# Three engines put into program order behind a matmul stream: chunk attention and a gated MLP on one core

## The chip, the core and the metric

The kernel runs on one core of a Trainium2 chip. The core has a matrix engine (TensorE, in the profile PE, its weight loads PEld), a vector engine (VectorE, DVE), an activation engine (ScalarE, ACT), a general one (GpSimd, POOL) and one that here only issues transfers (SyncE, SP; its queue is SPq). Each takes its instructions in the order of its own list; semaphores tie the lists together. Matmuls read SBUF and write PSUM. The metric is the device time of one execution in microseconds (us).

## What is computed

The inputs are q, k and v (8 batches, 8 heads, 576 tokens, head size 64), two weights of 512 x 1536, one of 1536 x 512 and a norm's gain g of 512.

```python
# attention inside chunks of 64 tokens, per head
scores = q_c @ k_c.T / sqrt(64); scores -= max(scores)
attn = exp(scores) / (sum(exp(scores)) + 1e-9)
x = attn @ v_c                        # as [4608 tokens, 512]
# root mean square norm and gated MLP
xn = x / sqrt(mean(x * x) + 1e-6) * g
h = silu(xn @ w_gate) * (xn @ w_val)  # [4608, 1536]
out = h @ w_out                       # [4608, 512]
```

All is float32. Every wide product is made of three matmuls of a reduced form: an operand is split into a high half (a cast) and a low half (operand minus high half), and high x high, high x low and low x high are summed. So each operand costs a cast (ScalarE) and a subtraction (VectorE).

## The kernel before, in words

The 4608 tokens are 9 tiles of 512; attention goes by units of 256 tokens, so two units make a tile, four a pair of tiles. Tiles 0, 1 and 2 are done plainly: for each f of 12 (128 columns of the middle size) `gated` makes the gate and the value product (`up`, 24 matmuls), silu on ScalarE (line 523), the product on VectorE (line 527), the high half gh (line 528) and the low half gl (line 532); then `down` of the f before adds 12 matmuls into four accumulators. The other 6 tiles are three pairs, done by a scheme with seven products instead of eight, named P1 to P7: `up_pair` runs 6 times per pair, with 7 products of 12 matmuls each; `after` evacuates each product (copies on ScalarE, sums on VectorE, products on GpSimd). `down_pair` then runs 42 pieces (7 products x 6) of 6 matmuls; each piece needs a split of its token operand, gh on ScalarE (line 829) and gl on VectorE (line 830), made by `split_next` one piece ahead.

The attention of later tiles lies between these matmuls. A unit is a list of steps (`unit_steps`): load q, k, v; scores on TensorE (line 244) with the softmax (`turned_softmax`: a reduction and a subtraction, each twice per half unit, and the exp); sums, a transposition on VectorE and a store (`turn`); the load that brings the tiles home turned (`turn_back`, the tile eT); the values on TensorE (line 366) and the norm (`turned_norm`, with the square and its sum on ScalarE, `inv_rms` with the power -1/2 on GpSimd, line 433, and the scale on ScalarE, line 388); the turned x to memory (`turn_x`, line 394) and back (`turn_x_back`). `Steps` holds a table: at which step which of these functions runs. Tile two has 24 half steps (two per f), a pair has 84 (42 products up, 42 pieces down); the constants UNIT_AT, UNIT_STEPS, PAIR_AT, PAIR_STEPS place the units. The same tables hold `out_sides` (in tile two: sums and splits of the output weights for the pairs, stored to memory) and `x_sides` (scale by g, line 676, sums, line 679, and splits, lines 662 and 663, of a pair's x into the seven operands xp). Weights of the pairs come from memory as tiles wr (up, three ahead) and wo (down, three ahead), through SP's queue like every transfer.

What sets the order: from tile one on a manual schedule holds TensorE's list in program order (line 1012). The lists of ScalarE, VectorE, GpSimd and SP come from a scheduler that goes by priority and its own estimates; `urgent()` lifts the priority of an evacuation or a split.

Buffers that matter: `io` has 4 (q, k, v of a unit and its xu), `gp` 2 each for gh and gl, `tmp` 4, `xs` 8, `wts` 18 large ones (xp, wr, wo, g, tt), PSUM two banks each for `ps_h` and `ps_a`, four for `ps_acc`.

## Time and profile before

| | |
|---|---|
| median of 3 runs | 935.68 us (932.73 to 936.3) |
| profiled execution, its own time | 935.86 us |
| span from first to last instruction | 934.0 us |
| mean granted clock of TensorE | 0.993 |
| tile two, 258.24 to 375.73 | 117.5 us |
| first pair, 375.73 to 567.01 | 191.3 us |
| second pair, 567.01 to 756.64 | 189.6 us |
| third pair (no attention left), 756.64 to the end | 177.4 us |
| transfers | 231.85 MB, mean 248 GB/s |

The stretches are read from TensorE's rows: each starts with its first wide matmul. A row of the timeline gives start, length, engine, line, operation, the tiles (written <- read), shapes and a count of merged instructions; a bracket at its end tells how long the engine sat idle before it and what ended that. A row of the table of waits gives engine, line and tile, what it waited for, the total in us, how often and the longest.

### The profile page before, as it was taken

The numbers are of one execution on the slowest core, as the hardware profiler recorded it, in microseconds if no ns is written. First come the engines' busy times: TensorE is split into PE (matmuls) and PEld (weight loads), VectorE is DVE, ScalarE is ACT, GpSimd is POOL, SyncE is SP. The second block draws the span as 40 slices with busy tenths as digits, with TensorE's granted clock in tenths as the row PEclk, the third lists the DMA queues.
The fourth block names the chain that finished last, engine by engine and source line by source line (L and its number), as shares of the span: only waits on it lengthen the run. The fifth ranks groups of instructions, "written<-read, shape, count | busy, mean of one in ns | idle before, by whom it ended". The sixth has DMA issues, their size and how long they took to land.

```text
span 934.0 us, 17571 instructions
## 1 busy us (share of the span) xinstructions
PE 892.4 (96%) x6828; PEld 726.1 (78%) x6828; DVE 637.0 (68%) x1065; ACT 470.8 (50%) x779; POOL 186.7 (20%) x161
## 2 busy tenths in 40 slices
PE   5699989999999989999998999999999999999997
PEld 4478868888888778888886888888877888888786
DVE  5899983654578783975775996666859954333775
ACT  4989853443456543744453654354636632322453
POOL 0100012224300000143333001443320013332201
PEclk9999999999999999999999999999999999999999
DMA  8688998778876766677796686777777675345801
GB/s 343 243 316 303 331 325 281 244 252 249 294 288 230 229 183 202 250 276 262 237 323 241 240 331 210 283 260 241 267 273 258 241 273 229 135 153 206 340 23 69
DMA packets 85795, 231.85 MB, mean 248 GB/s; under 512 B 8912, under 2 KB 45264, under 8 KB 71504
## 3 DMA queue, kind: packets, MB, share of 16 engines
q1 hardware_dynamic: 85712, 230.72, 70.3%
q8 instruction: 54, 0.88, 0.4%
q14 instruction: 29, 0.24, 0.1%
HBM read 167.25 MB, written 63.44 MB: 247 GB/s over the span
## 4 chain that ended last, share of the span: by engine, by line
PE 76%; issue 7%; ACT 6%; DVE 6%; POOL 2%; DMA 1%; SPq 0%; DVEq 0%; ACTq 0%; POOLq 0%
PE ps_c L722 11%; PE ps_a L722 11%; PE ps_b L722 10%; PE ps_g L505 7%; PE acc L540 7%; PE ps_v L505 7%; PE ps_b L911 5%; PE ps_d L722 5%; PE ps_c L911 4%; PE ps_d L911 3%; PE ps_a L911 3%; PE ps_o L366 2%; PE ps_s L244 2%; DVE gl L830 1%; ACT w L157 1%
## 5 line engine op out<-in xcount | busy, mean ns | idle before, releaser
L722 PE MATMUL ps_b<-xp,wr 128*128 128x512 f32 x432 | 106.0, 395 | 0.0
L722 PE MATMUL ps_c<-xp,wr 128*128 128x512 f32 x432 | 104.6, 391 | 0.0
L505 PE MATMUL ps_g<-xh,parts 128*128 128x512 f32 x288 | 98.1, 400 | 5.9 <-ACT sg L523 5.1
L722 PE MATMUL ps_a<-xp,wr 128*128 128x512 f32 x432 | 103.5, 390 | 0.0
L505 PE MATMUL ps_v<-xh,parts 128*128 128x512 f32 x288 | 96.0, 393 | 0.0
L722 PEld LDWEIGHTS ps_b<-xp,wr 128*128 128x128 f32 x432 | 81.7, 190 | 17.4
L722 PEld LDWEIGHTS ps_a<-xp,wr 128*128 128x128 f32 x432 | 80.9, 188 | 16.9
L722 PEld LDWEIGHTS ps_c<-xp,wr 128*128 128x128 f32 x432 | 80.6, 188 | 17.0
L540 PE MATMUL acc<-parts,gh 128*128 128x512 f32 x288 | 90.8, 396 | 0.0
L829 ACT CAST gh<-g 128x512 fp32r<-128x512 f32 x72 | 44.6, 623 | 51.8 <-DVE gl L830 21.0
L505 PEld LDWEIGHTS ps_g<-xh,parts 128*128 128x128 f32 x288 | 55.0, 191 | 19.5 <-ACT sg L523 6.4
L505 PEld LDWEIGHTS ps_v<-xh,parts 128*128 128x128 f32 x288 | 54.7, 190 | 11.5
L540 PEld LDWEIGHTS acc<-parts,gh 128*128 128x128 f32 x288 | 53.5, 189 | 11.6 <-ACT parts L182 0.2
L801 POOL TENSOR_TENSOR g<-u,u 128x512 f32<-128x512 f32 x18 | 23.2, 1289 | 185.8 <-ACT u L769 72.1
L830 DVE TENSOR_TENSOR gl<-g,gh 128x512 fp32r<-128x512 f32 x72 | 49.3, 700 | 12.2 <-ACT gh L829 11.9
L505 PE MATMUL ps_g<-xl,parts 128*128 128x512 f32 x144 | 57.0, 396 | 0.0
L540 PE MATMUL acc<-parts,gl 128*128 128x512 f32 x144 | 56.4, 392 | 0.0
L505 PE MATMUL ps_v<-xl,parts 128*128 128x512 f32 x144 | 56.4, 392 | 0.0
L791 POOL TENSOR_TENSOR p<-p,p 128x512 f32<-128x512 f32 x36 | 46.9, 1318 | 42.8 <-DVE p L790 33.5
L769 ACT ACTIVATE p<-p 128x512 f32<-128x512 f32 x36 | 22.6, 632 | 64.4 <-POOL p L791 61.2
L433 POOL TENSOR_TENSOR ri<-ss,mhalf 128x1 f32<-128x1 f32 x32 | 19.6, 623 | 173.6 <-DVE ss L431 173.5
L527 DVE TENSOR_TENSOR sg<-ps_v,sg 128x512 f32<-128x512 f32 x36 | 24.7, 686 | 42.0 <-PE ps_v L505 35.0
(141 smaller groups left out, 1794.9 us busy)
## 6 DMA issues: line engine op xcount, KB each, us to landing
wr<-wsd SPq DMA_DIRECT2D x63, 1024.0 KB, 6.8
wo<-osd SPq DMA_DIRECT2D x30, 1024.0 KB, 7.8
raw<-w_up_dram SPq DMA_DIRECT2D x12, 1024.0 KB, 9.6
vt<-v_dram SPq DMA_DIRECT2D x18, 512.0 KB, 5.2
wsd<-parts SPq DMA_DIRECT2D x18, 512.0 KB, 7.0
qt<-qT_dram SPq DMA_DIRECT2D x17, 512.0 KB, 4.9
kt<-kT_dram SPq DMA_DIRECT2D x17, 512.0 KB, 5.8
away_e<-e SPq DMA_DIRECT2D x28, 256.0 KB, 2.4
```

The costliest lines, as they stand in the source:

```text
L244: nc.tensor.matmul(st["s"][j][c * CH : (c + 1) * CH, pr], st["q"][rows, pr, tok : tok + CH], st["k"][rows, pr, tok : tok + CH], start=True ...
L433: nc.gpsimd.tensor_tensor(ri, ss, mhalf, op=ALU.pow)
L505: nc.tensor.matmul(ps, a[f][:, cols], b[dt], start=(dt == 0 and i == 0), stop=(dt == NDT - 1 and i == 2),)
L527: nc.vector.tensor_tensor(sg, pv, sg, op=ALU.mult)
L540: nc.tensor.matmul(acc[s], a[:, cols], b, start=(f == 0 and i == 0), stop=(f == NF - 1 and i == 2),)
L722: nc.tensor.matmul(ps, w[:, a, m, cols], xp[:, b, kt], start=start and kt == 0 and i == 0, stop=stop and kt == 1 and i == 2, skip_group_ch ...
L769: nc.scalar.activation(t, t if src is None else src, AF.Silu)
L791: nc.gpsimd.tensor_tensor(kp["p5"], kp["p1"], kp["p5"], op=add)
L801: nc.gpsimd.tensor_tensor(g[:, 0, 1], kp["u2"], kept[0]["u2"], op=mult)
L829: nc.scalar.copy(gh, src)
L830: nc.vector.tensor_tensor(gl, src, gh.bitcast(F32), op=ALU.subtract)
L911: nc.tensor.matmul(banks[m][name], w[:, a, m * P : (m + 1) * P], b, start=opens and i == 0 and k == 0, stop=not (opens and p != P4) and i ...
```

## The change

From tile two on the manual schedule covers TensorE, ScalarE, VectorE and SP (not GpSimd); tile one keeps TensorE alone. So what the text says last runs last on each of these engines, and the tables of steps are dealt anew in smaller pieces:

- a unit has 12 steps: the two exps stand together behind both softmaxes (one step later in the pairs), the halves of a unit go away and come home separately, and the norm is three steps: the product with the square sums of both halves (`turned_norm`), the root (`turned_root`: one VectorE and one GpSimd instruction on two columns instead of two on one), the scale (`turned_scale`);
- in tile two the first half step of an f runs inside `gated`, between the high and the low half of that f; `out_sides` comes in four smaller lists from step 0 on; the load of the pairs' first weights goes from half step 14 to 18; the first unit's load goes to the end of tile one;
- `x_sides` is dealt as single casts and subtractions; the scale by g goes from VectorE to ScalarE; the operands P3, P6, P7 and P4 (and in tile two P5's low half) are made in the first four products of the pair that uses them;
- the two sums at the end of `up_pair` run behind the second product of the next one, the last ones behind piece 1 of the down phase;
- the down phase's high halves are made two pieces ahead, in `tmp` tiles, the low halves one ahead; the first two high halves and the first low one inside the last up product; the copy of P2's result goes to an `xs` tile; at the last piece of a product the matmuls go by bank, first all of one, then all of the other;
- `urgent()` goes where the order is now that of the text.

```diff
 UNIT_AT = 1, 5, 9, 13
-UNIT_STEPS = -2, 0, 1, 3, 5, 6, 7
-FIRST_STEPS = -2, 0, 1, 3, 7, 8, 9
-PAIR_STEPS = -4, 0, 3, 5, 8, 11, 13
-PAIR_AT = 2, 12, 21, 31
+UNIT_STEPS = -3, 0, 0, 1, 1, 2, 2, 5, 6, 6, 7, 8
+FIRST_STEPS = -2, 0, 0, 1, 1, 3, 3, 7, 7, 7, 8, 9
+PAIR_STEPS = -4, 0, 1, 2, 3, 4, 4, 8, 9, 10, 11, 12
+PAIR_AT = 3, 12, 22, 31
+OUT_AT = 3
+X_AT = 5, 12, 13, 14, 15, 16, 25, 27, 30
+IN_ORDER = {
+    mybir.EngineType.PE,
+    mybir.EngineType.Activation,
+    mybir.EngineType.DVE,
+    mybir.EngineType.SP,
+}
...
+    def turned_exp(i):
+        e = state[i]["e"]
         nc.scalar.activation(e, e, AF.Exp, scale=SCALE)
...
+    def turned_norm(u):
+        xu = state["xu", u] = io.tile([P, 4, NDT, 2, Q], F32, tag="io", name="xu")
+        xv = xu.rearrange("p q a s d -> p s (q a) d")
+        ss = state["ss", u] = small.tile([P, 2], F32, name="ss_u")
+        for s in range(2):
+            st = state.pop(2 * u + s)
+            nc.vector.tensor_tensor(
+                xv[:, s].rearrange("p (h b) d -> p h b d", b=2),
+                st["o"].rearrange("p (h b d) -> p h b d", b=2, d=Q),
+                st["rs"].rearrange("p h (o i) -> p h o i", i=1).broadcast_to([P, H, 2, Q]),
+                op=ALU.mult,
+            )
+            spent = st["eT"].rearrange("p t h q -> p (t h) q")
+            nc.scalar.activation(spent, xv[:, s], AF.Square, accum_out=ss[:, s : s + 1])
+    def turned_root(u):
+        ss = state["ss", u]
+        nc.vector.tensor_scalar(ss, ss, 1.0 / DM, 1e-6, op0=ALU.mult, op1=ALU.add)
+        ri = state["ri", u] = small.tile([P, 2], F32, name="ri_u")
+        nc.gpsimd.tensor_tensor(ri, ss, mhalf.broadcast_to([P, 2]), op=ALU.pow)
+    def turned_scale(u):
+        xv = state["xu", u].rearrange("p q a s d -> p s (q a) d")
+        ri = state.pop(("ri", u))
+        for s in range(2):
+            nc.scalar.mul(xv[:, s], xv[:, s], ri[:, s : s + 1])
...
+        if between is not None:
+            between()
         with urgent():
             nc.vector.tensor_tensor(gl, sg, gh.bitcast(F32), op=ALU.subtract)
         return gh, gl
...
+        return [
+            [join, sums_one],
+            [lambda: split(P7, (2, 1)), sums_two],
+            [lambda: split(P5, (2, 2)), lambda: split(P6, (1, 1))],
+            [lambda: split(P3, (1, 2))],
+        ]
     def save_plain(i):
...
+        def high(p):
+            xside[p] = big([P, 2, 2, TT], F32R, "xp")
+            hi, _, x = views(p)
+            nc.scalar.copy(hi, x)
+        def low(p):
+            hi, lo, x = views(p)
+            nc.vector.tensor_tensor(lo, x, hi.bitcast(F32), op=ALU.subtract)
...
         def scale(x, dts):
             for dt in dts:
                 col = g_col[:, dt : dt + 1]
-                nc.vector.tensor_scalar(x[:, :, dt], x[:, :, dt], col, None, op0=ALU.mult)
+                nc.scalar.mul(x[:, :, dt], x[:, :, dt], col)
...
+        late = [
+            [lambda: less(got["t1"], b22, got["t1"]), lambda: high(P3), lambda: high(P6)],
+            [lambda: low(P6), lambda: less(b12, b22, b12), lambda: low(P3), lambda: high(P7)],
+            [lambda: low(P7), lambda: less(b21, got["t1"], b21), lambda: high(P4)],
+            [lambda: low(P4)],
+        ]
+        return one, two, late
     ring = {}
...
                 product(n, m, p, b, p in (P1, P6, P5, P4), p in (P2, P7, P3, P4))
-            with urgent():
-                after(p, ps, kept, g)
+            if k == 6 and last is not None:
+                last()
+            after(p, ps, kept, g)
+            if k == 1 and sums:
+                sums.pop()()
             step()
...
+        def sum_up():
+            nc.vector.tensor_tensor(t, g[:, 0, 1], g[:, 0, 0], op=ALU.subtract)
+            nc.vector.tensor_tensor(g[:, 0, 1], g[:, 1, 1], g[:, 0, 1], op=ALU.subtract)
+        sums.append(sum_up)
...
+    def split_high(src, ready):
+        gh = tmp.tile([P, TT], F32R, tag="tmp", name="gh")
+        nc.scalar.copy(gh, src)
+        ready.append([gh])
+    def split_low(src, pair):
+        gl = gp.tile([P, TT], F32R, name="gl")
+        nc.vector.tensor_tensor(gl, src, pair[0].bitcast(F32), op=ALU.subtract)
+        pair.append(gl)
...
+        def next_high(n):
+            if n < len(order):
+                split_high(source(n), ready)
+        def next_low(n):
+            if n >= len(order):
+                return
+            split_low(source(n), ready[n])
...
-            split_next(n + 1)
-            gh, gl = ready.pop(n)
+            next_high(n + 2)
+            next_low(n + 1)
+            gh, gl = ready[n]
             w = wos[n // PER][:, n % PER]
-            for k, (a, b) in enumerate(((0, gh), (1, gh), (0, gl))):
-                for m in range(2):
-                    nc.tensor.matmul(
-                        banks[m][name],
-                        w[:, a, m * P : (m + 1) * P],
-                        b,
-                        start=opens and i == 0 and k == 0,
-                        stop=not (opens and p != P4) and i == NPR - 1 and k == 2,
-                        skip_group_check=True,
-                    )
+            todo = [(m, k) for k in range(3) for m in range(2)]
             if i == NPR - 1:
-                with urgent():
-                    finish(p, banks, kept)
+                todo.sort()
+            for m, k in todo:
+                nc.tensor.matmul(
+                    banks[m][name],
+                    w[:, (0, 1, 0)[k], m * P : (m + 1) * P],
+                    (gh, gh, gl)[k],
+                    start=opens and i == 0 and k == 0,
+                    stop=not (opens and p != P4) and i == NPR - 1 and k == 2,
+                    skip_group_check=True,
+                )
+            if i == NPR - 1:
+                finish(p, banks, kept)
+            if n == 1:
+                sums.pop()()
             step()
     def unit_steps(u, x):
...
+        def second():
+            turned_softmax(both[1])
             for i in both:
-                turned_softmax(i)
-
-        def second():
-            for i in both:
-                turned_sum(i)
-                turn(i)
-
-        def third():
-            for i in both:
-                turn_back(i)
-
-        def fourth():
+                turned_exp(i)
...
             lambda: load_unit(u),
             first,
             second,
-            third,
-            fourth,
+            lambda: away(both[0]),
+            lambda: away(both[1]),
+            lambda: turn_back(both[0]),
+            lambda: turn_back(both[1]),
+            values,
+            lambda: turned_root(u),
+            lambda: turned_scale(u),
             lambda: turn_x(u),
             lambda: turn_x_back(u, x),
         ]
...
+            at.setdefault(21, []).append(lambda: load_unit(2 * PLAIN))
         elif t == 2:
+            ordered.__exit__(None, None, None)
             st = last.open("st2", 1)
             x2 = st.tile([P, NSUB, DM], F32, tag="x2", bufs=1, name="x2")
-            at = {}
+            ordered = tc.manual_schedule(engines=IN_ORDER)
+            ordered.__enter__()
             for n, u in enumerate(range(2 * PLAIN, 2 * PLAIN + 4)):
                 for k, f in enumerate(unit_steps(u, (x, x2)[n // 2])):
-                    at.setdefault(max(UNIT_AT[n] + UNIT_STEPS[k], 0), []).append(f)
+                    if n or k:
+                        at.setdefault(UNIT_AT[n] + UNIT_STEPS[k], []).append(f)
...
+            one, two, late = x_sides(x, x2, st)
+            for n, f in enumerate(one):
                 at.setdefault(15 + n, []).append(f)
-            for n, f in enumerate(x_both):
-                at.setdefault(22 + n // 6, []).append(f)
-            at.setdefault(14, []).append(lambda: ring_load_ahead(0))
-            half = Steps(at)
+            at.setdefault(23, []).extend([two[0], two[4], *two[1:3]])
+            late = [[two[3]] + late[0], *late[1:]]
+            at.setdefault(18, []).append(lambda: ring_load_ahead(0))
+            early = {n: list(todo) for n, todo in enumerate(late)}
...
+            one, two, late = x_sides(x, x2, st)
+            for n, f in enumerate(one[:2]):
+                at.setdefault(PAIR_AT[1] + PAIR_STEPS[-1] + 2 + n, []).append(f)
+            for n, f in zip(X_AT, one[2:] + two[:1] + two[4:] + two[1:4]):
+                at.setdefault(7 * NPR + n, []).append(f)
+            early = {n: list(todo) for n, todo in enumerate(late)}
         step = Steps(at)
         gts, wos, tt = [], [], []
+        sums, ready = [], []
+        def first_splits():
+            for g, _ in gts[:2]:
+                split_high(g[:, 0, 0], ready)
+            split_low(gts[0][0][:, 0, 0], ready[0])
         for i in range(NPR):
-            gts.append(up_pair(i, step, wos, tt))
+            last_part = first_splits if i == NPR - 1 else None
+            gts.append(up_pair(i, step, wos, tt, sums, last_part))
         loaded[0] = 0
-        down_pair(t, gts, wos, step, b + 1 < NB)
+        down_pair(t, gts, wos, step, b + 1 < NB, sums, ready)
     ordered.__exit__(None, None, None)
     last.close()
```

More of the change, by code (lines that the diff above doesn't have):

```diff
@@ L512, in up, with gated @@
         return ps
-    def gated(f, at, then):
+    def gated(f, at, then, between=None):
         pg = up(wgh, wgl, f, "ps_g")
@@ L655, in big @@
         return wts.tile(shape, dtype, tag="wts", name=name)
-    def x_side(p, src):
-        t = xside[p] = big([P, 2, 2, TT], F32R, "xp")
-        hi, lo = (t[:, i].rearrange("p k (n c) -> p k n c", c=2 * Q) for i in range(2))
-        src = src.rearrange("p n k c -> p k n c")
-        nc.scalar.copy(hi, src)
-        nc.vector.tensor_tensor(lo, src, hi.bitcast(F32), op=ALU.subtract)
     xside = {}
@@ L732, in hold, with up_pair @@
         return xs.tile([P, TT], F32, tag="xs", name=name)
-    def up_pair(i, step, wos, tt):
+    def up_pair(i, step, wos, tt, sums, last=None):
         g = big([P, 2, 2, TT], F32, "g")
@@ L837, in out_load, with down_pair, source @@
         return t
-    def down_pair(t, gts, wos, step, more):
+    def split_high(src, ready):
[6 more added lines that the diff above has]
+        pair.append(gl)
+    def down_pair(t, gts, wos, step, more, sums, ready):
         order = [(p, i) for p in DOWN for i in range(NPR)]
-        ready = {}
         add, sub = ALU.add, ALU.subtract
-        def split_next(n):
-            if n >= len(order):
-                return
+        def source(n):
             p, i = order[n]
             g, tt = gts[i]
-            src = {
+            return {
                 P1: g[:, 0, 0], P5: tt, P2: g[:, 1, 0], P6: tt,
@@ L853, in split_next @@
             }[p]
-            ready[n] = split_g(src)
+        def next_high(n):
[5 more added lines that the diff above has]
+            split_low(source(n), ready[n])
+            p, i = order[n]
+            g, tt = gts[i]
             if p == P5:
@@ L875, in finish @@
                 elif p == P2:
-                    o = tmp_tile("o")
+                    o = hold("o")
                     nc.scalar.copy(o, b["a"])
@@ L931, in first, with away, values @@
                 scores(i, sc)
+            turned_softmax(both[0])
+        def second():
+            turned_softmax(both[1])
             for i in both:
[L933 to L944 removed]
+                turned_exp(i)
+        def away(i):
+            turned_sum(i)
+            turn(i)
+        def values():
             turned_values(u)
[L946 to L947 removed]
+            turned_norm(u)
         return [
```

103 lines of the change are left out of this document (33 added, 70 removed).

## The prediction

> **What bounds the kernel now.** I read the page first, then TensorE's timeline from tile two on, the table of waits for that stretch, and last the rows of the other engines around each stall.
>
> ```profile
> span 934.0 us, 17571 instructions
> PE 892.4 (96%) x6828; PEld 726.1 (78%) x6828; DVE 637.0 (68%) x1065; ACT 470.8 (50%) x779; POOL 186.7 (20%) x161
> ```
>
> TensorE is busy for 892.4 of 934.0 us, so the change can only win what TensorE loses. What a stretch should cost I take from a place without stalls. A row gives its start, its length, the engine, the line and the count.
>
> ```profile
> 572.29 2.88 PE L722 MATMUL ps_c<-xp,wr 128*128 128x512 f32 x12
> 575.10 1.16 PE L244 MATMUL ps_s<-kt,qt 64*64 64x64 f32 x64
> 576.19 3.02 PE L722 MATMUL ps_b<-xp,wr 128*128 128x512 f32 x12
> ...
> 598.18 1.48 PE L366 MATMUL ps_o<-vt,eT 64*32 64x64 f32 x128
> 599.59 3.02 PE L722 MATMUL ps_c<-xp,wr 128*128 128x512 f32 x12
> ```
>
> Twelve wide matmuls start at 572.29 and the next thing at 575.10, so twelve cost about 2.72 us when others follow at once: the same pitch as six in 1.36. The scores of a unit take 576.19 - 575.10 = 1.09 us, its values 599.59 - 598.18 = 1.41 us. All this work stays. What is not in this beat are the waits; each row of their table has the total in us, the count and the longest.
>
> ```profile
> PE ps_a L911 <- DVE gl L830: 6.0, 7, 1.6
> PE ps_o L366 <- DMA eT<-away_e: 1.9, 2, 1.6
> ...
> PEld ps_a L911 <- DVE gl L830: 9.5, 8, 2.1
> ```
>
> Nearly all the waiting from 258 us on is of two kinds: the first split halves of a down phase (gl, line 830) and the values of a unit (line 366). VectorE and ScalarE are not full over the span (68% and 50%). They are late at places, by the order in which their work was laid out.
>
> **Part one: values that come too late.** Each pair of rows gives the start of the values (or of what they delay) and of the work behind them.
>
> ```profile
> 307.85 0.27 PE L366 MATMUL ps_o<-vt,eT 64*32 64x64 f32 x2 [0.33 <-DMA eT<-away_e]
> 310.86 0.73 PE L540 MATMUL acc<-parts,gh 128*128 128x512 f32 x2
> ...
> 328.88 0.27 PE L366 MATMUL ps_o<-vt,eT 64*32 64x64 f32 x2
> 333.05 1.22 PE L540 MATMUL acc<-parts,gh 128*128 128x512 f32 x2
> 337.34 0.50 PE L505 MATMUL ps_g<-xh,parts 128*128 128x512 f32 x1 [0.59 <-ACT sg L523]
> ...
> 351.17 2.58 PE L366 MATMUL ps_o<-vt,eT 64*32 64x64 f32 x128
> 353.68 0.73 PE L540 MATMUL acc<-parts,gh 128*128 128x512 f32 x2
> ...
> 495.03 1.47 PE L366 MATMUL ps_o<-vt,eT 64*32 64x64 f32 x127
> 498.76 4.42 PE L722 MATMUL ps_b<-xp,wr 128*128 128x512 f32 x12
> 503.02 2.90 PE L722 MATMUL ps_d<-xp,wr 128*128 128x512 f32 x12
> ...
> 656.43 2.19 PE L366 MATMUL ps_o<-vt,eT 64*32 64x64 f32 x128
> 658.54 3.01 PE L722 MATMUL ps_b<-xp,wr 128*128 128x512 f32 x12
> ```
>
> Against 1.41 us the values at 307.85 take 3.01, at 328.88 4.17, at 351.17 2.51, at 495.03 3.73, at 656.43 2.11. Lost: 1.60 + 2.76 + 1.10 + 2.32 + 0.70 = 8.5 us. Twice the twelve matmuls behind are slow too: 333.05 to 337.34 is 4.29 us (with a 0.59 wait inside), 498.76 to 503.02 is 4.26 us, against 2.72: 1.57 + 1.54 = 3.1 us. In the second case the clock shows it (the third-last column is the granted clock):
>
> ```profile
> 494.00:504.00 10.00, 7.97 (x150) 6.21 (x149) 4.65 (x9) 2.25 (x6) 2.77 (x3) 0.83 0.83 347
> ```
>
> The change brings the tiles of a unit home earlier: in tile two turn_back comes 2 half steps after the scores instead of 3, with the values left at 5; in the pairs the store of the first half comes at 2 instead of 3 steps, turn_back at 4 instead of 5, with the values left at 8. One pair step is 2.72 us, a half step of tile two about 4.1 us (8.16 / 2). The largest lateness above is 2.76 us. So I book all 8.5 us and the 3.1 us of slow clock that follow from them as won.
>
> **Part two: the first pieces of a down phase.**
>
> ```profile
> 694.27 1.07 PE L911 MATMUL ps_a<-gh,wo 128*128 128x512 f32 x4
> ...
> 706.32 1.07 PE L911 MATMUL ps_c<-gh,wo 128*128 128x512 f32 x4
> ...
> 508.11 1.24 DVE L394 STREAM_TRANSPOSE xu<-xu 128x1024 f32<-128x1024 f32 x1
> 510.44 2.31 DVE L663 TENSOR_TENSOR xp<-x,xp 128x1024 fp32r<-128x1024 f32 x1
> ```
>
> The first product of the down phase has six pieces of six matmuls, 8.16 us by the beat; from 694.27 to 706.32 it takes 12.05. Meanwhile VectorE works at 510.44 (the same place one pair earlier) on an operand of the next pair, an instruction that the scheduler put between two splits, after the turned x at 508.11. The change makes the first two high halves and the first low half inside the last up product, always keeps the high half two pieces ahead and the low half one, and leaves on VectorE among the first six pieces only the subtraction of line 803, the last unit's turned x (1.24) and two sums. A low half is due 0.91 us into its piece of 1.36. With 0.65 us for every subtraction (1.29 for the two of line 890, below), piece 1's is ready at 0.65 + 0.65 = 1.3 of 2.27 us, piece 2's, behind the turned x, at 3.2 of 3.63, piece 3's, behind the sums, at 5.2 of 4.99: 0.2 us late, say 0.4 with the handing over, in the two phases that have units. TensorE's own waits of this kind are 6.0 us, those of its weight queue 9.5 us; the loss at 694.27 alone is 3.89 us, so the truth is near the upper one: 9.0 us won. The 0.4 in two phases, 0.8 us, goes to what is added; if VectorE comes 1 us late in each of three phases it is 3.0.
>
> **Part three: the tail.**
>
> ```profile
> 928.42 0.61 PE L911 MATMUL ps_d<-gl,wo 128*128 128x512 f32 x2
> 928.92 1.29 DVE L890 TENSOR_TENSOR p<-p,ps_d 128x512 f32<-128x512 f32 x2 [1.67 <-PE ps_d L911]
> ```
>
> Both last subtractions wait for the last matmul. Sorting the last piece by bank closes the first bank three matmuls (0.68 us) earlier; the one behind it then has only itself to wait for. 0.7 us won; the store behind it is unchanged.
>
> **Part four: moved work that should cost nothing.** The scale by g goes from VectorE to ScalarE, 24 instructions (minimum, median and maximum in ns):
>
> ```profile
> L676 DVE TENSOR_SCALAR x<-x,g_col x24: 432/480/1520, 332.5 to 717.7; 128x512 f32<-128x512 f32 x24
> L388 ACT ACTIVATE xu<-xu,ri x28: 707/722/727, 198.9 to 694.6; 128x512 f32<-128x512 f32 x28
> ```
>
> VectorE loses 24 x 0.48 = 11.5 us, ScalarE gets 24 x 0.72 = 17.3 us. It lies in the down phases and at the end of tile two; ScalarE, busy for half the span, covers it; without cover the price is at most 17.3 us, of which 5.8 are more than VectorE paid. [...] The delayed sums, the split of out_sides and the high half in another pool add no instruction and no transfer. The two exps of a unit now stand together, which saves table loads at best; booked at zero.
>
> **Part five: what program order adds.** Now an engine whose head waits holds everything behind it.
>
> ```profile
> 258.00:376.00 118.00, 114.32 (x1204) 93.05 (x1203) 84.18 (x179) 60.64 (x102) 5.24 (x8) 0.99 0.69 221
> ...
> L315 DVE TENSOR_TENSOR e<-ps_s,mx 128x256 f32<-128x256 f32 x56 | 21.0, 412 | 0.0
> L679 DVE TENSOR_TENSOR t<-x,x 128x1024 f32<-128x1024 f32 x3 | 3.7, 1218 | 0.0
> ```
>
> In tile two VectorE is busy for 84.18 of 118 us, but unevenly: the softmax of a unit is 4 x (0.41 + 0.41) = 3.3 us (the reduction taken like the subtraction) at one half step, and between half steps 6 and 14 softmax, away, norm and out_sides of several units meet, while the first and last f have one unit or none. I estimate 46 us of VectorE's 84 in the five f from 3 to 7, where TensorE needs 5 x (8.16 + 2.50 / 2) = 47. There a wait of VectorE isn't made good. turned_root and turned_scale stand in one half step: ScalarE holds scale until POOL's root is done (0.55 to 1.0 us), works 2 x 0.72, and only then makes the copy on which VectorE's next split waits: about 2.5 us idle. Behind ScalarE's scale stands the next silu, on that the PSUM bank of TensorE. The first and last unit have slack; for two units I book 2 x 2.5 = 5.0 us. The bounds are 0 and 4 x 2.5 = 10.0; no gain below zero, as the waits of before are already booked. At the start of a pair the late operands come in: before P6 (5.44 us after P1, as P2 and P5 lie between) VectorE has t1's difference (1.22), a product that waits for a silu behind two casts, and P6's low half (1.22). That ends about when it is due: 0.4 us for each of three, 1.2 us; bounds 0 and 3 x 1.22 = 3.7. SP's moved transfers cost nothing while weights are three tiles ahead.
>
> **Sum.** The profiled execution took 935.86 us, 1.86 more than its span and 0.18 more than the median of 935.68. Won: 8.5 + 3.1 + 9.0 + 0.7 = 21.3. Added: 5.0 + 1.2 + 0.8 = 7.0. 935.86 - 21.3 + 7.0 = 921.6, so 922.
>
> **Rivals.** *Nothing is added:* the waits fit in the slack and the time is 935.86 - 21.3 = 914.6. For it: VectorE is busy for 68% of the span; against: the 46 of 47 us above.
>
> *ScalarE waits for the root in order (slower).* The root is now one instruction on two columns per unit, not two on one.
>
> ```profile
> 126.55 3.94 POOL L470 TENSOR_TENSOR ri_u<-ss_u,mhalf 128x2 f32<-128x2 f32 x1 [41.45 <-DVE ss_u L468]
> ...
> 129.25 0.69 DVE L167 TENSOR_SCALAR w<-w 128x1024 int32<-128x1024 int32 x1
> ...
> 130.53 0.72 ACT L472 ACTIVATE x<-x,ri_u 128x512 f32<-128x512 f32 x1 [4.50 <-POOL ri_u L470]
> ...
> L433 POOL TENSOR_TENSOR ri<-ss,mhalf x32: 543/551/1951, 17.1 to 693.9; 128x1 f32<-128x1 f32 x32
> ```
>
> This two-column case took 3.94 us and ended at 130.49, 0.55 us after VectorE's row at 129.25, which stands without idle time behind its forerunners; ScalarE's scale waited 4.50 us with a silu behind it. Against it stand 32 single-column ones with a median of 0.55 us. If twelve units from tile two on pay this, the four of tile two cost 4.5 us each and the eight in the pairs, where scale comes one step (2.72 us) later, 1.8 each: 32.4 us, 954. The time is slower by 0.5% (940.4) from (940.4 - 921.6) / 12 = 1.6 us per unit. [...]
>
> *SP's queue.* Four io buffers hold q, k, v and xu. In tile two the load of a unit now comes two half steps before the turned x of the unit two earlier has left, and its v finds no buffer. The text order can't be kept strictly there, as the transfer that frees the buffer stands behind it.
>
> ```profile
> eT<-away_e SPq DMA_DIRECT2D x112, 64.0 KB, 3.3
> away_x<-xu SPq DMA_DIRECT2D x14, 512.0 KB, 3.7
> ```
>
> If turn_back stands behind that v, it starts after 3.7 us of the other transfer and lands 3.3 us on, at a point where two half steps (8.2 us) are all there is: about 2.5 us late for three units, plus 1.5 us of slow clock each, 12 us: 934. That would be no change.
>
> **How the numbers follow.** This kernel's three runs span 0.4%, so 0.5% (4.7 us) is about what can be told from nothing: under 931.0 is faster, over 940.4 slower. Forecast 0.58, nothing added 0.20, SP's queue 0.12, the root 0.10. So faster 0.78, same 0.12, slower 0.10. The range reaches down past 914.6 by the few us by which unquoted small waits could add, to 911, and up past 931 (21.3 won, 10.0 + 3.7 + 3.0 added) and the SP case to 936, which leaves the slower case out.
>
> **What would show it.** Right: no wait of a down phase's first pieces on gl; values of 1.41 us throughout; no stretch of granted clock under 0.9 after 258 us; ScalarE's scale waiting for POOL and VectorE for the split's cast in tile two, with TensorE waiting there for a few us in all; tile two still over its beat, the pairs nearly on it. Wrong: waits of 4 us at the scale, weights (wr, wo) among TensorE's waits, or the values still late.

## The result and the profile after

The changed kernel takes 957.07 us (median of 4 runs, 953.39 to 959.79) against 935.1 in the same session: ratio 1.0239, 95% interval 1.0217 to 1.0261, 2.4% slower. The profiled execution took 954.95 us. Its page, the span, the engines and the start of the chain of work that ended last:

```profile
span 953.2 us, 17568 instructions
PE 897.7 (94%) x6828; PEld 726.7 (76%) x6828; DVE 640.1 (67%) x1027; ACT 460.8 (48%) x787; POOL 180.8 (19%) x147
PE 58%; DMA 12%; DVE 11%; issue 8%; ACT 7%; SPq 2%; POOL 1%; DVEq 0%; ACTq 0%; POOLq 0%
```

No engine has noticeably more to do; TensorE executes the same 6828 matmuls. The chain tells more: DMA is now 12% of it (1% before). TensorE's waits from 258 us on:

```profile
PE ps_o L377 <- DVE e L323: 6.9, 4, 5.5
PE ps_b L757 <- DMA wr<-wsd: 4.3, 3, 2.0
PE ps_s L252 <- issue: 4.1, 3, 1.7
PE ps_o L377 <- DMA away_x<-xu: 3.2, 1, 3.2
...
PEld ps_a L964 <- DVE gl L880: 4.8, 8, 0.8
```

The first pieces of the down phases wait less for gl (weight queue 4.8 against 9.5). The values (line 377) still wait, now behind the softmax (line 323); weights (wr) and scores without a named cause are new. The granted clock is the third-last column here: it dipped to 0.96 in tile two, the first stretch.

```profile
254.73:383.15 128.42, 115.57 (x1202) 93.39 (x1200) 79.85 (x164) 54.14 (x99) 2.78 (x4) 0.96 0.56 186
383.15:581.71 198.56, 189.96 (x1525) 152.47 (x1524) 140.42 (x222) 95.56 (x157) 45.83 (x36) 0.98 0.70 255
581.71:776.47 194.76, 188.16 (x1525) 151.35 (x1524) 138.10 (x220) 92.12 (x151) 45.85 (x36) 0.99 0.70 257
776.47:953.20 176.73, 172.42 (x757) 141.40 (x755) 102.59 (x137) 60.94 (x100) 44.08 (x32) 1.00 0.49 185
```

Where the time went follows from TensorE's rows: each group from its start to the next one's, less the prediction's beat. Loss above the beat in us (the two right columns are experiments told below):

| | before | after | TensorE alone in order (3) | the best kernel (17) |
|---|---|---|---|---|
| tile two | 9.4 | 20.4 | 2.8 | 6.1 |
| first pair, up | 5.9 | 14.9 | 17.5 | 4.6 |
| first pair, down | 4.0 | 2.3 | 1.8 | 2.8 |
| second pair, up | 3.1 | 10.8 | 5.5 | 1.8 |
| second pair, down | 5.1 | 2.6 | 3.9 | 3.9 |
| third pair with its tail | 6.1 | 5.3 | 5.6 | 5.6 |
| sum from tile two on | 33.6 | 56.3 | 37.1 | 24.8 |

22.7 us are lost net. (Up to the end of tile zero all kernels told of here run the same code, and yet tile one begins at 149.5 to 157.5 us in their profiles. So I count from tile two on. A stage starts here with the start of its first wide matmul; the table ahead of the change took the end of the matmul before it for the pairs, about 0.16 us later, hence 117.5 there and 117.3 below.)

In tile two it begins on SyncE's queue. These rows of the timeline are from all engines, unrelated ones left out:

```profile
297.18 0.38 SPq L221 DMA_DIRECT2D kt<-kT_dram  x1
...
301.75 1.16 PE L252 MATMUL ps_s<-kt,qt 64*64 64x64 f32 x64
...
302.98 0.33 SPq L222 DMA_DIRECT2D vt<-v_dram  x1
...
303.71 0.56 SPq L624 DMA_DIRECT2D osd<-side  x1
...
304.37 3.76 SPq L360 DMA_DIRECT2D eT<-away_e  x8
...
307.86 0.41 ACT L622 CAST side<-wo 128x256 fp32r<-128x256 f32 x1 [3.38 <-DMA osd<-side]
...
308.30 0.43 DVE L623 TENSOR_TENSOR side<-wo,side 128x256 fp32r<-128x256 f32 x1 [3.32 <-ACT side L622]
...
309.24 0.42 DVE L322 TENSOR_REDUCE mx<-ps_s 128x4 f32<-128x256 f32 x1
...
311.80 0.27 PE L377 MATMUL ps_o<-vt,eT 64*32 64x64 f32 x2 [3.21 <-DMA away_x<-xu]
312.06 0.42 DVE L323 TENSOR_TENSOR e<-ps_s,mx 128x256 f32<-128x256 f32 x1
312.59 1.82 PE L377 MATMUL ps_o<-vt,eT 64*32 64x64 f32 x126 [0.52 <-DVE e L323]
```

The queue stands from 297.6 to 302.98: v finds no buffer until the unit's own scores have freed one. It happens to two units of tile two, for 11.1 us in all. In the queue's own waits this is in two rows, one for the time until q has landed and one for the time until the scores have read it:

```profile
SPq L222 <- PE ps_s L252: 5.8, 2, 3.2
SPq L222 <- DMA qt<-qT_dram: 5.3, 2, 2.8
```

Behind v stand a store (osd) and the turn-back. ScalarE's cast needs the buffer of a stored part and waits 3.38 us, VectorE's subtraction waits for the cast, and the softmax, whose scores were done at 301.75 + 1.09 = 302.84, begins at 309.24. The values of the unit before need the two banks that the softmax reads: two of their 128 matmuls start at 311.80, the others at 312.59, 0.11 us after the softmax's last subtraction (312.06 + 0.42). The store that the row at 311.80 names carries another unit's x; the values don't read it.

In the pairs the same queue, up to the wide matmuls that wait:

```profile
502.43 7.60 SPq L360 DMA_DIRECT2D eT<-away_e  x8
510.12 0.37 SPq L749 DMA_DIRECT2D wr<-wsd  x1
...
515.15 4.12 PE L757 MATMUL ps_b<-xp,wr 128*128 128x512 f32 x10 [2.02 <-DMA wr<-wsd]
```

A weight load stands 7.6 us behind eight turn-backs.

### The profile page after: what moved, and what is told of

Read it like the earlier page. It is cut to its first block, busy times and chain, and to the rows that moved or that the text cites. A ratio compares the mean times of both kernels' runs of the same rounds, so it can differ in the third digit from the quotient of the medians.

```text
span 953.2 us, 17568 instructions
## 1 busy us (share of the span) xinstructions
PE 897.7 (94%) x6828; PEld 726.7 (76%) x6828; DVE 640.1 (67%) x1027; ACT 460.8 (48%) x787; POOL 180.8 (19%) x147
## 4 chain that ended last, share of the span: by engine, by line
PE 58%; DMA 12%; DVE 11%; issue 8%; ACT 7%; SPq 2%; POOL 1%; DVEq 0%; ACTq 0%; POOLq 0%
PE acc L564 6%; PE ps_b L757 6%; PE ps_c L757 6%; PE ps_a L757 6%; PE ps_g L527 6%; PE ps_v L527 5%; PE ps_c L964 5%; PE ps_b L964 5%; DMA wr<-wsd 5%; PE ps_a L964 4%; PE ps_d L757 4%; PE ps_d L964 2%; DMA osd<-side 2%; PE ps_o L377 1%; DMA away_e<-e 1%
## 5 line engine op out<-in xcount | busy, mean ns | idle before, releaser
L880 DVE TENSOR_TENSOR gl<-g,gh 128x512 fp32r<-128x512 f32 x72 | 52.2, 731 | 18.8 <-PE ps_c L964 6.0
L527 PE MATMUL ps_v<-xl,parts 128*128 128x512 f32 x144 | 56.3, 391 | 0.0
L811 ACT ACTIVATE p<-p 128x512 f32<-128x512 f32 x36 | 22.7, 632 | 68.4 <-POOL p L833 47.9
L757 PE MATMUL ps_d<-xp,wr 128*128 128x512 f32 x216 | 52.7, 393 | 2.8 <-DVE u L839 1.8
```

Source lines behind the costliest of these rows:

```text
L527: nc.tensor.matmul(ps, a[f][:, cols], b[dt], start=(dt == 0 and i == 0), stop=(dt == NDT - 1 and i == 2),)
L757: nc.tensor.matmul(ps, w[:, a, m, cols], xp[:, b, kt], start=start and kt == 0 and i == 0, stop=stop and kt == 1 and i == 2, skip_group_ch ...
L811: nc.scalar.activation(t, t if src is None else src, AF.Silu)
L880: nc.vector.tensor_tensor(gl, src, pair[0].bitcast(F32), op=ALU.subtract)
```

## The experiments

"All in order" means TensorE, ScalarE, VectorE and SyncE's queue. Ratios are to the kernel before on the same chip. Stage times are from one profiled execution each, whose span stands beside the median; that of 10 took 6.5 us less than its median, that of 13 4.9 us more.

| kernel | median us | ratio, 95% interval | span | tile two | pair 0 | pair 1 |
|---|---|---|---|---|---|---|
| before | 935.1 | | 934.0 | 117.3 | 191.3 | 189.6 |
| after | 957.07 | 1.0239 (1.0217 to 1.0261) | 953.2 | 128.4 | 198.6 | 194.8 |
| 1 SyncE free | 942.34 | 1.0079 (1.0052 to 1.0107) | 944.7 | 115.4 | 201.2 | 190.4 |
| 2 VectorE, ScalarE free | 940.82 | 1.0059 (1.0033 to 1.0084) | 938.5 | 113.8 | 198.0 | 191.4 |
| 3 all three free | 935.68 | 1.0005 (0.9984 to 1.0025) | 937.0 | 110.7 | 200.6 | 190.8 |
| 4 v and turn-backs later | 976.9 | 1.043 (1.0392 to 1.0467) | 978.2 | 118.2 | 215.7 | 213.1 |
| 5 v later | 950.15 | 1.0172 (1.0137 to 1.0208) | 951.5 | 118.1 | 200.7 | 198.9 |
| 6 v later, four wr ahead | 953.1 | 1.0193 (1.0153 to 1.0234) | 954.3 | 118.5 | 206.1 | 194.6 |
| 7 as 3, tile two's units earlier | 936.51 | 1.0019 (1.0001 to 1.0036) | 934.4 | 113.6 | 200.0 | 188.7 |
| 8 as 3, pair units 2, 12, 22, 32 | 934.6 | 0.9998 (0.9979 to 1.0016) | 932.4 | 111.1 | 197.6 | 191.4 |
| 9 osd stores on GpSimd | 950.35 | 1.014 (1.0096 to 1.0184) | 952.3 | 120.5 | 202.7 | 196.8 |
| 10 v later in tile two | 950.1 | 1.0141 (1.0092 to 1.019) | 941.9 | 118.2 | 195.4 | 198.3 |
| 11 as 10, four wr ahead in up | 938.41 | 1.0046 (1.0016 to 1.0077) | 936.9 | 118.1 | 193.8 | 191.1 |
| 12 as 7, operands in tile two | 932.31 | 0.9964 (0.9942 to 0.9985) | 933.8 | 114.0 | 192.0 | 189.2 |
| 13 as 11, q and k earlier | 936.92 | 1.003 (1.0002 to 1.0058) | 940.0 | 115.1 | 200.4 | 192.4 |
| 14 as 13, pair units 2, 12, 22, 32 | 935.86 | 0.9998 (0.9975 to 1.0022) | 932.4 | 115.1 | 192.9 | 191.0 |
| 15 as 13, scale later | 936.52 | 1.0026 (0.9994 to 1.0058) | 934.8 | 112.8 | 193.7 | 191.7 |
| 16 as 12, pair units 2, 12, 22, 31 | 929.0 | 0.9934 (0.9905 to 0.9963) | 927.8 | 114.3 | 189.5 | 188.8 |
| 17 as 12, pair units 1, 11, 21, 31 | 924.93 | 0.9897 (0.987 to 0.9925) | 922.4 | 114.0 | 188.9 | 187.1 |
| 18 as 15, pair units 2, 12, 22, 31 | 934.8 | 1.0008 (0.9979 to 1.0038) | 932.1 | 112.8 | 193.8 | 191.8 |

### Which order costs (1 to 4)

```diff
 IN_ORDER = {
     mybir.EngineType.PE,
-    mybir.EngineType.Activation,   # 2 and 3
-    mybir.EngineType.DVE,          # 2 and 3
-    mybir.EngineType.SP,           # 1 and 3
 }
```

Expected of 1, SyncE free:

> SyncE's queue is taken out of the set of engines in program order; everything else is the changed kernel (957.07). Theory Q (SyncE's queue in program order is the cause: a load of v with no buffer, and turn-back loads that wait for a store, hold the queue, and the stores, weights and inputs behind them come late): the waits of ps_b and ps_c for wr go, the values in tile two are 1.41 us again, tile two falls from 128.4 to about 116 and pairs 0 and 1 from 198.6 and 194.8 to about 190: 921 to 932. Rival H (the order of VectorE and ScalarE is the cause: softmax, scales and evacuations stand behind others that wait): the late values stay, 945 to 957.

Expected of 2, VectorE and ScalarE free:

> VectorE and ScalarE are taken out of the set; TensorE and SyncE's queue stay in program order. Theory Q: most of the loss stays, 947 to 960, with wr among TensorE's waits. Rival H: the loss goes, 925 to 938.

Expected of 3, all three free:

> Only TensorE is in program order, as before, with the new step tables and the finer pieces. It stands beside the one without SyncE: the difference of the two is what the order of VectorE and ScalarE brings by itself. Theory Q: 921 to 937, no wr waits. Rival H: also 921 to 937, but then the kernel without SyncE alone must be far above it. A third theory (the new steps, not the order, lose the time) says about 955 here.

The order of SyncE's queue alone costs 940.82 - 935.68 = 5.1 us, that of VectorE and ScalarE alone 6.7, both together 21.4: 9.6 more than the sum. 1 and 2 each ended between what Q and what H had said, and neither theory holds alone. Theory Q is half right: the queue has to be held and VectorE and ScalarE have to be unable to go round what it holds. Rival H alone is out (VectorE and ScalarE in order without SyncE: 942.34, not 945 and more), and kernel 3 rules out the new steps as the cause (935.68, not 955). But the new steps bring nothing either: tile two is 6.6 us shorter than before and pair 0 9.3 longer. The rows of kernel 3 there:

```profile
368.79 5.60 PE L754 MATMUL ps_a<-xp,wr 128*128 128x512 f32 x24
377.27 0.51 PE L754 MATMUL ps_c<-xp,wr 128*128 128x512 f32 x1 [2.88 <-ACT xp L700]
378.66 5.06 PE L754 MATMUL ps_c<-xp,wr 128*128 128x512 f32 x11 [0.88 <-DVE xp L704]
383.52 3.65 PE L754 MATMUL ps_b<-xp,wr 128*128 128x512 f32 x12
```

P5 (ps_c) is due at 374.23 and starts at 377.27; from there to the next product pass 6.25 us, 0.88 of them a wait, where the beat is 2.72. With P6 7.4 us are lost at once.

Kernel 4 keeps all in order, moves v's load behind the unit's own scores (from unit 6 on) and both turn-backs of a pair's unit:

```diff
-PAIR_STEPS = -4, 0, 1, 2, 3, 4, 4, 8, 9, 10, 11, 12
+PAIR_STEPS = -4, 0, 1, 2, 3, 6, 6, 8, 9, 10, 11, 12
...
-        nc.sync.dma_start(vt, v[u])
...
             for i in both:
                 scores(i, sc)
+            load_values(u)
```

Expected of 4:

> SyncE's queue stays in program order, but two things that stop it are moved: from unit 6 on the load of v is issued behind the unit's own scores instead of with q and k, and in the pairs the two turn-backs come at step 6 instead of 4. Theory Q: nothing else is needed, tile two about 117 and the pairs about 190, so 922 to 935. Rival H: no change, 950 to 957. If only the length of the queue counts and not what stops it, it also stays above 945.

A miss by 42 us, and useful: tile two came down by 10.2 us, the pairs rose by 17 and 18. TensorE's largest wait there:

```profile
PE ps_o L383 <- DMA eT<-away_e: 22.4, 16, 4.2
```

Here a step of the ordered queue was a place, not a time: two steps later was two steps of weights later, and the turned rows missed the values.

### The two moves apart, and the given-back gain (5 to 8)

5 is kernel 4 without the line of PAIR_STEPS, 6 adds a tile of lead; 7 and 8 are kernel 3 with one line each.

```diff
-AHEAD_R = 3                    # 6
+AHEAD_R = 4
-UNIT_AT = 1, 5, 9, 13          # 7
+UNIT_AT = 0, 4, 8, 12
-PAIR_AT = 3, 12, 22, 31        # 8
+PAIR_AT = 2, 12, 22, 32
```

Expected of 5:

> All three queues in program order, with one edit: from unit 6 on the load of v is issued behind the unit's own scores. In the kernel with both moves tile two came down from 128.4 to 118.2 us and the pairs rose to 215.7 and 213.1, with 22.4 us of values that waited for turned rows. Theory V (v's load that finds no buffer is what costs tile two its 11 us; the turn-backs at step 6 alone cost the pairs theirs): tile two about 118, pair 0 about 198, pair 1 about 195 as in the changed kernel, 945 to 949. Rival (v behind the scores is itself what makes the pairs late): pairs near 215, about 975.

Expected of 6:

> As the kernel with only v's load moved, and the weights of the pairs' up phase are loaded four tiles ahead instead of three. Theory W (in the pairs a wr load stands behind a turn-back that waits up to 7.9 us for its store, and three tiles of lead do not cover it): TensorE's waits for wr, 5.9 us in all in the changed kernel, and the slow clock behind them go, 937 to 942. Rival R (the loads then only stand elsewhere in the same queue: the fourth tile finds no buffer and holds the queue itself): no gain over the kernel with only v moved, 945 to 955.

Expected of 7:

> Only TensorE in program order, and the four units of tile two one half step (4.7 us) earlier. With only TensorE in order tile two fell to 110.7 us and pair 0 began with 7.4 us of waits for its P5 operands, whose tokens came back at about 373. Theory C (the chain of tile two's last unit, not TensorE, sets when pair 0 can go on, so what tile two gains pair 0 gives back): the waits at pair 0's start fall by 4 to 5 us or go, 929 to 932. Rival (a half step earlier meets VectorE and ScalarE at the same work and gains nothing, or the values in tile two come late): 934 to 938.

Expected of 8:

> Only TensorE in program order, and the units of a pair at steps 2, 12, 22, 32 instead of 3, 12, 22, 31, so that two steps lie between the values of one unit and the scores of the next in every case, not in one of three. Theory I (scores that come one step behind the values stall in their middle because TensorE's next block of instructions is only then being fetched: 1.9 us without a releaser, a 16 KB instruction packet at 414.5 and at 474.3): scores take 1.09 us throughout, 3 to 6 us less in the two pairs, 930 to 933. Rival (the stall is a wait for the banks that the values hold, or for q and k): it stays, 934 to 938.

Tile two is 118.1 us in 5: theory V holds there, though only 6.9 of its 10 us reach the end; the last units' values stalled (4.3 and 5.8 us over the beat in the two pairs). In 6 TensorE never waits for wr, but for wo, which now stands behind four wr of the next pair; rival R holds there. TensorE's largest wait of 6, and its queue at the end of a down phase:

```profile
PE ps_d L970 <- DMA wo<-osd: 7.3, 2, 4.3
```

```profile
561.28 2.11 SPq L755 DMA_DIRECT2D wr<-wsd  x4
563.49 0.61 SPq L876 DMA_DIRECT2D wo<-osd  x1
```

7 is a miss: the operands of P5 came no earlier. Its transfers from 350 to 370 us (KB each, median us from issue to landing) show why: the turned x landed after 11.2 us, beside 3.7 us for it in the prediction's row.

```profile
away_x<-xu SPq DMA_DIRECT2D x1, 512.0 KB, 11.2
```

Three wr tiles had been issued right ahead of it:

```profile
348.54 1.40 SPq L746 DMA_DIRECT2D wr<-wsd  x3
349.99 0.83 SPq L416 DMA_DIRECT2D away_x<-xu  x1
```

In 8 the stalled scores went (5.2 us to none) as theory I has it, and first pieces of down waited 7.8 us for gl instead.

### The way from the held queue to TensorE (9 to 12)

```diff
-            nc.sync.dma_start(out_home(i, p), part...)      # 9
+            nc.gpsimd.dma_start(out_home(i, p), part...)
-            lambda: load_unit(u),                           # 10, 11: v later in tile two alone
+            lambda: load_unit(u, not 2 * PLAIN <= u < 2 * PLAIN + 4),
-        while loaded[0] < min(n + AHEAD_R, len(wsd)):       # 11, with AHEAD_R = 4
+        while loaded[0] < min(n + (AHEAD_R if n else 3), len(wsd)):
-            at.setdefault(18, []).append(lambda: ring_load_ahead(0))   # 12
+            at.setdefault(14, []).append(lambda: ring_load_ahead(0))
-            at.setdefault(23, []).extend([two[0], two[4], *two[1:3]])
+            at.setdefault(22, []).extend([two[0], two[4], *two[1:4], *late[0]])
+            at.setdefault(23, []).extend([*late[1], *late[2], *late[3]])
```

Expected of 9:

> The changed kernel, all three queues in program order, v's load where it was; only the stores of the down weights' parts (osd) are issued by GpSimd instead of SyncE. Theory S (the held queue costs tile two through these stores: the parts keep their buffers, ScalarE's next cast waits up to 5.5 us for a store, VectorE's subtraction and the softmax stand behind it): the casts no longer wait, tile two falls from 128.4 to about 118, 945 to 949. Rival E (the held queue costs through the turned rows that come late to the values): the values still wait, tile two above 125, 953 to 958.

Expected of 10:

> The changed kernel with v's load behind the scores in tile two's four units alone; the pairs as changed. Tile two 118 as in the two kernels that moved v in all units; pairs 198.6 and 194.8 as changed, without the 8.2 us of values without a releaser that those had at the fourth unit: 945 to 949. If that wait has another cause than v's place, 950 as with v moved everywhere.

Expected of 11:

> As the kernel with v moved in tile two alone, and four tiles of weights ahead in the up phase only, three at the change from down to up, so that down's own last tiles keep their buffers (with four there, wo came 7.3 us late at the ends of the down phases). Theory W: neither wr nor wo is waited for, pair 0 about 195 and pair 1 about 190, 937 to 943. Rival R (the fourth tile's load holds the queue for a buffer): another load or the turned rows come late, 945 to 952.

Expected of 12:

> Only TensorE in program order, tile two's units one half step earlier as before, and now the work that turned out to stand by its place in the program: the pairs' first weights are loaded at half step 14 as in the kernel before (18 in the changed one), and the token operands for P5, P6, P3, P7 and P4 are made at half steps 22 and 23 instead of in pair 0's first steps. Theory C2 (what tile two gains is given back at pair 0's start, 7.4 us, because these operands are placed there and their tokens wait in the DMA queues behind 4 MB of weights, q and k): the waits for xp at pair 0's start go, pair 0 about 193, 928 to 931. Rival (VectorE and ScalarE have no room at tile two's end, so the wait moves to tile two's last steps): 934 to 937.

9 leaves v where it holds the queue and takes only the stores out from behind it. ScalarE's wait for them in tile two, after and in 9:

```profile
ACT side L622 <- DMA osd<-side: 12.4, 3, 5.5
```

```profile
ACT side L622 <- DMA osd<-side: 1.7, 1, 1.7
```

Tile two falls by 7.9 of the 10 us, the median by 6.7: theory S, not rival E, though the median stays a little above the 945 to 949 that S had said. 10 ends where 5 did: its pair 1 has a stall of 4.1 us in values again, so v's place was not the cause of that. 11 mends both losses of the queue with everything still in order: 957.07 to 938.41. Its pair 0 and 1 are 193.8 and 191.1, no wr is waited for, and wo for 0.8 us: theory W. But of the 8.8 us by which its two pairs are shorter than those of 10, only 4.0 are the waits for wr that 10 has (2.6 + 0.9 + 0.5); 4.9 are stalls of values that 11 has less of, and that W doesn't speak of. 12 shows the given-back gain: with its weights loaded before the last turned x and its operands made in tile two, pair 0 is 8.0 us shorter than in 7 and tile two 0.4 longer (the last two turned x landed after 3.4 us, the median); of this 4.2 us show in the medians, just short of the expected 928 to 931.

### What remained (13 to 18)

```diff
-UNIT_STEPS = -3, 0, 0, 1, 1, 2, 2, 5, 6, 6, 7, 8
+UNIT_STEPS = -4, 0, 0, 1, 1, 2, 2, 5, 6, 6, 7, 8     # 13, 14
+UNIT_STEPS = -4, 0, 0, 1, 1, 2, 2, 5, 6, 7, 7, 8     # 15, 18
```

PAIR_AT is as the table says.

Expected of 13:

> As the kernel with v moved in tile two and four tiles ahead (938.41), and q and k of a unit of tile two are loaded one half step earlier, ahead of the previous unit's stores of its turned exponentials instead of behind them. Theory K (k's load stands behind stores that wait for VectorE, so scores wait 1.9 us three times): those waits go, tile two from 118.1 to about 112 to 113, 932 to 934. Rival (the load now finds no buffer and holds the queue itself): tile two 118 or more, 938 or more.

Expected of 14:

> As the one with the earlier q and k, and the pairs' units at steps 2, 12, 22, 32, two steps between one unit's values and the next one's scores in each case. With only TensorE in order this took the stalled scores away (5.2 us without a releaser to none) but the down phase's first pieces then waited 7.8 us for gl. Theory I with the order of VectorE (the pieces cannot be overtaken now): 3 to 5 us less than the kernel without it, 928 to 931. Rival (the last unit's work again meets the first pieces of down): no gain, 932 to 935.

Expected of 15:

> As the one with the earlier q and k, and in tile two the scale by the root comes one half step later, so that ScalarE doesn't stand 4 to 6 us for the root. The prediction put 5.0 us of tile two on that wait. If that term holds: tile two 4 to 5 us shorter than without it, 928 to 930. If ScalarE's idle time there is off the path, as TensorE's waits suggest (none of them is for the scale): within 1 us of the kernel without it, or 1 to 2 us longer since the turned x leaves later.

Expected of 16:

> Only TensorE in order, with tile two as in the kernel that makes its operands early (932.31), and the pairs' units at 2, 12, 22, 32. Theory I: the 3.7 us of stalled scores go, and what the first pieces of down then wait for gl (7.8 us with the same steps before) takes the place of the 2.1 us: 930 to 935, no clear gain. If gl does not wait, 927 to 929.

Expected of 17:

> Only TensorE in program order, tile two as in the kernel that makes its operands early, and the pairs' units at steps 1, 11, 21, 31. In the kernel before this one (929.0) they stood at 2, 12, 22, 31, not at 32 for the last as its expectation has it; its last unit came one step behind the third's values and its scores stalled, 1.66 and 1.53 us, with an instruction packet 0.2 and 0.7 us ahead of them, while the six others took 1.09. Theory I (the fetch): with two steps between values and scores everywhere all eight scores take about 1.1 us and the last unit is no later, so gl does not wait either, 925 to 928. Rival (q and k, or some other operand, are what the stalled scores wait for): one step less of lead makes it worse, 930 or more.

Expected of 18:

> All three queues in program order with every mend so far (v in tile two behind the scores, q and k one half step earlier, the scale one half step later, four tiles of weights ahead in the up phase), and the pairs' units at 2, 12, 22, 31, which takes the stalls of two of four scores away without making the last unit later. From the one with the later scale (936.52): 2 us per pair with units, 931 to 934. Rival (the order has cost in other places that move along): 935 or more, that is, no better than before even when mended.

13: scores no longer wait for k (4.8 to 0.4) and tile two is 3.0 us shorter, but the median moves by 1.5, inside the noise: K holds for tile two, not for the end. (Pair 0 is 6.6 us longer than in 11, and 4.9 of these are one stall of values at 497.67, again without a releaser.) 15: the later scale shortens tile two by another 2.3; the medians differ by 0.4. 14 and 18: no gain that can be told from none; all in order and mended, this kernel stands at before's time (1.0008). 16 ran with 31 for the last unit, not the 32 of its expectation, so it says nothing on the 32. With its interval wholly under 1, as that of 12 was, it gains 0.7% on before, and 17 gains most: all eight scores of the pairs took their beat, as theory I had it, the median is at the lower end of what it said, and the kernel is 1.0% faster than before.

## Why the prediction was wrong

**The step that failed** is "SP's moved transfers cost nothing while weights are three tiles ahead." Taking SyncE's queue out of the order gives back 957.07 - 942.34 = 14.7 us; mending what held it (11) 18.7, with fewer stalls of values in it. The rival *SP's queue* had the right place (v's load that finds no buffer) and too small a price, 12 us on a won 21.3. It followed the turn-backs to the values alone; the dearer way went by the stores behind the load: parts' buffers, ScalarE's cast, VectorE, softmax (9 took 7.9 us away by moving those stores alone). And it looked at tile two only; in the pairs weights stood behind the turn-backs (4.0 us of waits for wr in 10, none in 11). The order of VectorE and ScalarE by itself cost 6.7 us (1 against 3), near the 7.0 that the sum adds; as the terms below came out otherwise, that is luck.

**Late values, 8.5 and 3.1 us.** For tile two the booking was right as far as it went: 6.6 us won with TensorE alone in order (9.4 to 2.8). With TensorE alone in order it was given back in pair 0: 7.4 us in kernel 3, 8.0 shown by 12, where the sum had 1.2 us for late operands, 3.7 at most. In the changed kernel itself no operand was late there. Its first two products of pair 0 lost 1.7 us, and the wait named is for an evacuation by ScalarE:

```profile
387.39 3.01 PE L757 MATMUL ps_a<-xp,wr 128*128 128x512 f32 x12 [1.37 <-ACT p L817]
```

So the 1.2 us booked for late operands were not paid there. Why the operands are late in 3 and not here, no run isolates. The 2.32 + 1.54 us at 495.03 were not lateness either. That row has 127 of the 128 matmuls, and no releaser is named for the last:

```profile
498.52 0.31 PE L366 MATMUL ps_o<-vt,eT 64*32 64x64 f32 x1 [2.03 <-issue]
```

Kernel 3 has the same stall at the same unit, 2.25 us ahead of the last matmul at 503.08 (more on it in the last section).

**First pieces of down, 9.0 us.** The table's losses of the down phases fell from 10.1 (4.0, 5.1 and 1.0 in the third) to 5.7 (2.3, 2.6 and 0.8): 4.4 won, a mis-sized term. It could not have been 9.0: above the beat the three first products had lost 2.8, 3.9 and 1.0 us, 7.7 in all, and the 9.5 us that the sum went by are waits of the weight queue, of which TensorE lost less. After the change they lose 1.6, 1.7 and 0.8. In the first product of pair 1's down phase two pieces start 1.91 and 2.01 us after the one before instead of 1.36, with 0.34 us named:

```profile
719.93 1.20 PE L964 MATMUL ps_a<-gh,wo 128*128 128x512 f32 x4
721.27 0.73 PE L964 MATMUL ps_a<-gl,wo 128*128 128x512 f32 x2
721.84 1.09 PE L964 MATMUL ps_a<-gh,wo 128*128 128x512 f32 x4
723.27 0.74 PE L964 MATMUL ps_a<-gl,wo 128*128 128x512 f32 x2 [0.34 <-DVE gl L880]
723.85 1.09 PE L964 MATMUL ps_a<-gh,wo 128*128 128x512 f32 x4
```

**Tail, 0.7 us.** Right: the last product's loss went from 5.1 to 4.5, 0.6 won.

**The root, 5.0 us and the 954 rival.** ScalarE waited longer for it than priced: 18.1 us over four units, 6.2 at most, because VectorE's small step ahead of it stood behind other work. The power itself is quick:

```profile
299.00 0.16 DVE L402 TENSOR_SCALAR ss_u<-ss_u 128x2 f32<-128x2 f32 x1
...
300.04 1.34 ACT L410 ACTIVATE xu<-xu,ri_u 128x512 f32<-128x512 f32 x2 [6.17 <-POOL ri_u L404]
...
L404 POOL TENSOR_TENSOR ri_u<-ss_u,mhalf x14: 690/700/1145, 194.2 to 716.3; 128x2 f32<-128x2 f32 x14
```

0.70 us in the median, 1.145 at most of 14, against the 3.94 of the one row the rival rested on; the rival was wrong in its price. Why that one row took 3.94, no run shows. How much of the 5.0 us was on the path: at most the 2.3 of tile two in 15, of which nothing shows in the medians.

**Not in the sum at all:** scores that stall, 5.5 us over the beat after against 1.0 before, by the new places of the units. The scale by g on ScalarE was moved back in no run, so its price stays untested. Table loads on ScalarE, booked at zero, fell from 23 to 15 at the exp, 1.28 us each.

The listed signs were good: "waits of 4 us at the scale, weights (wr, wo) among TensorE's waits, or the values still late" all came.

## What to carry to other kernels

Before a DMA queue is put into program order, write down for each of its transfers what it waits for (a buffer, a store, a cast) and what stands behind it; a load that waits for a buffer belongs behind the instruction that frees that buffer (v in 10: tile two from 128.4 to 118.2 us). Orders cost more together than apart here: one held queue and two engines that could not go round it cost 21.4 us, where each alone cost 5 to 7. A wait taken out of one stage is won only when the next stage's operands come as much earlier (kernel 3: tile two 6.6 us shorter, pair 0 9.3 longer); read the first groups of the next stage.

## What was unexpected of the hardware

TensorE stalls in the middle of a unit's scores or values without a releaser. Kernel 3, and the transfers of 414.4 to 415.4 us by kind (packets, MB, share):

```profile
414.56 0.50 PE L249 MATMUL ps_s<-kt,qt 64*64 64x64 f32 x17
416.98 0.93 PE L249 MATMUL ps_s<-kt,qt 64*64 64x64 f32 x47 [1.92 <-issue]
```

```profile
q8 instruction: 1, 0.02, 6.2%
```

That packet (16 KB; 54 in a run) starts at 414.50, and TensorE goes on 2.48 us later. In the packets' own times, over the profiles of all 20 kernels: of 160 groups of scores in the pairs 43 stall for over 1 us, and 40 of these have such a packet starting between 1.0 us ahead of their first matmul and 0.3 us behind it; of the 117 others 3 have. Values do the same, in before too: in the group at 495.03 the packet starts at 496.13 and TensorE goes on at 498.52, 2.39 us later. The best kernel, 17, still loses 2.3 us, but behind the group at 489.2, where the next matmul's row names a releaser (VectorE's xu, 2.23 us). In kernel 5:

```profile
502.45 1.50 PE L383 MATMUL ps_o<-vt,eT 64*32 64x64 f32 x125
507.82 0.42 PE L383 MATMUL ps_o<-vt,eT 64*32 64x64 f32 x3 [3.88 <-issue]
```

Here the packet itself starts only at 505.40, 1.5 us into the stall, and again 2.42 us pass. Values and scores are dense in instructions (128 and 64 short matmuls, each with a weight load, in 1.41 and 1.09 us; a wide matmul takes 2.72 / 12 = 0.23). With two steps of wide matmuls between them all eight groups of scores of 17 take their 1.09 us, one of them here:

```profile
435.95 1.16 PE L249 MATMUL ps_s<-kt,qt 64*64 64x64 f32 x64
437.04 1.19 PE L754 MATMUL ps_c<-xp,wr 128*128 128x512 f32 x4
```

That the fetch of instructions is the cause is inferred from these times. The distance between the groups goes with it: all 43 stalls are among the 62 groups of scores that stand one step behind values; none is among the 58 that stand two steps behind or the 40 of a pair's first unit. But a unit that is moved also meets the packets elsewhere. Only three groups two steps behind had a packet in that stretch (none of them stalled), so what the distance does by itself rests on these three. After the start of the packet TensorE goes on 2.39 to 2.48 us later in the three cases above, and 2.28 to 2.45 us later in the three groups of scores that stall in the changed kernel.
